# Where the q and k rows of one batch are transposed: TensorE or DMA, in an attention and MLP kernel

## The chip, the cores and the metric

The kernel runs on one core of a Trainium2 chip. The metric is the device time of one execution in microseconds (us). The core's engines are TensorE (PE, with its weight loads listed apart as PEld), VectorE (DVE), ScalarE (ACT), GpSimd (POOL) and SyncE (SP). Each works through its own queue in program order and waits on semaphores for the others. Loads are issued by POOL here, stores and DMA transposes by SP.

## The reference

Inputs are q, k and v of shape (8, 8, 576, 64), batch by head by position by head dimension, and two weight matrices of 512 x 2048 and 2048 x 512, all in float32.

```python
scores = (q @ k.T) / 8
mask_local = (rel >= 0) & (rel < 32)                       # heads 0..3
mask_strided = (rel >= 0) & (col % 32 == row % 32)         # heads 4..7
x = softmax(where(mask, scores, -1e9)) @ v                 # (8, 8, 576, 64)
x = x.transpose(0, 2, 1, 3).reshape(4608, 512)
out = relu(x @ w_in) ** 2 @ w_out                          # (4608, 512)
```

`rel` is the row's position less the column's. Heads 0 to 3 see the last 32 positions, heads 4 to 7 every 32nd one.

## The kernel before

**The MLP sets the rhythm.** The 4608 tokens are cut into nine chunks of 512. A chunk has 32 groups of four matmuls of 128x128 by 512 columns: 16 groups of the first product (`mm1`, line 709), then 16 of the second (`mm2`, line 731). So group 32c + i is step i of chunk c. After a group of mm1, ACT takes the rectified result out of PSUM (line 715) into one of four `r` tiles and DVE squares it (line 716). After every fourth group of mm2, ACT copies a tile `y` out (line 735) and SP stores it (line 739).

**Attention is threaded between the groups by hand.** The string `PLAN` gives, for each group number, the steps that are issued ahead of that group. Nothing reorders them: an engine's queue holds its instructions in the order in which the steps stand in `PLAN`. A chunk needs the attention of the tokens that it covers: chunk 2, from group 64 on, needs batch 2 (tokens 1152 to 1727), chunk 3, from group 96 on, batch 3.

**Units.** A pair of heads is a unit, numbered 4 x batch + pair: pairs 0 and 1 are local, 2 and 3 strided. Units 8 and 9 are batch 2's local pairs, units 12 and 13 batch 3's.

**The steps of a local unit:**

- *Load of q and k.* For batches 1 to 3 the step `l` (`load_qk_local_sw`, line 292) brings q or k of four heads in one DMA of 288 KB, six tokens in a row per partition, into columns of `xt` that are free at the time. `c` (`cast_qk_local`, line 299) rearranges a unit's part into a tile `q_l` or `k_l` of 96 partitions; the last letter names the engine (`a` ACT, `v` DVE). `T` (`step_T`, lines 455 and 462) transposes it with six PE transposes of 96 columns into a PSUM bank, from which ACT or DVE copies it to `qT` or `kTl`.
- From batch 4 on, `Q` (`load_qk_rows`, line 280) loads `q_l` or `k_l` directly, one token in a row, by two DMAs of 72 KB, one for each head. `Y` (`transpose_local`, line 380) issues two DMA transposes on SP, q first and then k. There are four buffers of `q_l` and four of `k_l`.
- *The rest.* `V` (`load_v_local_all`, line 420) loads the local v of a batch. `S` computes the scores (line 507), ACT their exponentials (line 523), and DVE multiplies them with the mask (line 529). `D` multiplies with v (line 669) and DVE divides (lines 674 and 675) into `x_l`. `E` transposes that into `xt`, from batch 2 on by a DMA transpose on SP (line 684).

**The steps of a batch's strided heads:** `C` (line 351) loads q or k rows into one tile for q and one for k, which every batch reuses. `X` (`transpose_str`, line 356) is their DMA transpose on SP into `qT_s` or `kT_s`. `k` (`step_K`, lines 367 and 370) spreads `kT_s` into the block matrix `kb`, one step for each of two halves. `U` (lines 392 and 395) loads v and `B` (line 399) spreads it into `vb`. `s` (`step_SS`, line 576, parts 0 to 2) computes the scores and `x` (`step_XX`, lines 587 and 590) the output, which DVE multiplies into `xt` (lines 600 and 606). With a batch number behind it, `X2k` is batch 2's transpose of k, `C3q` batch 3's load of q, `k30v` the first half of batch 3's spread of k, on DVE.

`o` (line 431) loads a quarter of the second weight matrix, and `m` clears a tile. An exclamation mark at `S` asks for all four exponentials at once.

Of the kernel before, what the change touches and what calls it, by code (L numbers as in the profile page):

```python
# [24 lines left out]
1: r1q mv1g  # L25
3: o0 mk1g
4: r1k V1
5: o1 U1 l2k8+9 mbg
6: o2 mv0g o3 mk0g V2
10: c4qv  # L30
11: c4kv
12: c5qv l2q8+9 T4qa
13: c5ka T4kv T5qa
14: W1q0v T5ka
15: S4
16: W1q1v
17: W1k0a W1k1v
18: S5! k10v
19: C2q C2k k11v D4.0
20: s1.0 D4.1 B10v  # L40
21: s1.1 D5.0
22: B11v l3k12+13 s1.2 U2
23: D5.1 x1.0
24: E4a
25: x1.1
26: X2k l3q12+13
27: x1.2
28: V3 E5a
29: c9kv
# [3 lines left out]
35: T8kv  # L53
37: T9kv
38: T8qv C3k
41: S8! k20v
42: T9qa B20v k21v
43: B21v
44: S9! D8.0 U3
45: D8.1  # L60
47: E8 D9.0
48: Q16k s2.0
49: D9.1
50: Q17q Q16q c12kv s2.1
51: c12qa E9 s2.2
52: Q17k c13kv c13qa
54: x2.0
55: X3q X3k
56: x2.1 C4k C4q
57: T12ka  # L70
58: V4 T13qv T12qa
59: T13ka
60: x2.2 B30v
61: B31v
63: U4 S12!
# [908 lines left out]
```

## Time and profile before

| what | us |
|---|---|
| median of three runs (301.77, 302.58, 1074.6) | 302.58 |
| the profiled execution | 301.36 |
| its span, from first to last instruction | 299.7 |
| matmuls of mm1 in the chain of waits (36% of the span) | 108 |
| matmuls of mm2 in the chain of waits (41% of the span) | 122 |
| ACT, line 715, 144 times | 85.5 |
| DVE, line 716, 144 times | 60.4 |

The page of the profile gives the share of busy time of each engine, the span in 40 slices, the DMA queues, the chain of work that ended last, and the costliest groups of instructions. The slices of PE, of its granted clock and of the DMA engines:

```profile
PE   7999999999999999999999999999999999999996
PEclk9999999999999999999999999999999999999999
DMA  7999999997999999999997998611011110010012
```

A digit is the share in tenths, and a slice is 7.5 us long. PE is busy throughout and has its full clock. The DMA engines are busy for the first 25 slices, in which all of q, k, v and the weights are loaded, and mostly idle after that. DMA transposes, loads and stores share them:

```profile
q0 software_dynamic: 54448, 18.82, 63.5%
q1 hardware_dynamic: 38512, 18.03, 30.0%
```

The columns are packets, MB, and the time that the packets took as a share of 16 engines' span. q0 holds POOL's loads, q1 the stores and the DMA transposes of SP.

In the lists of the trace, a line gives the start in us, the time in us, the engine, the line of the program, the operation, output and inputs, and in square brackets how long the engine was idle just before and what ended that.

### The profile page before, as it was taken

The page shows a single profiled execution, that of the slowest core. Times are in us where ns is not written, and L with a number is a line of the kernel's source. Part 1 is how long each engine was busy: PE and PEld are TensorE (multiplying, and loading weights), DVE is VectorE, ACT ScalarE, POOL GpSimd, SP SyncE. Part 2 cuts the span into 40 slices and gives each one's busy share as a digit, 9 for nine tenths or more (in the row PEclk, how much of TensorE's full clock was granted, in tenths as well). Part 3 has the DMA queues.
Part 4 walks back from the last instruction along what each step waited for, and adds up shares of the span by engine and source line. Part 5 has one row for each costly group of instructions (what it writes and reads, how often), then busy time and mean ns, then how long its engine had stood idle before and what let it go on. Part 6 is the DMA issues. An engine that isn't in the chain of part 4 may idle for free.

```text
span 299.7 us, 5685 instructions
## 1 busy us (share of the span) xinstructions
PE 292.3 (98%) x2172; PEld 145.7 (49%) x2172; DVE 180.2 (60%) x461; ACT 172.2 (57%) x324; POOL 71.7 (24%) x105
## 2 busy tenths in 40 slices
PE   7999999999999999999999999999999999999996
PEld 2554555544545444454454545444454444444444
DVE  5768699669668696589257945685485525104400
ACT  3758856685668744773467546645665356226511
POOL 8863933008204018047202900000000000000000
PEclk9999999999999999999999999999999999999999
DMA  7999999997999999999997998611011110010012
GB/s 146 190 210 201 191 200 185 157 231 112 141 131 182 172 156 199 151 141 179 204 162 112 161 205 119 108 56 71 35 23 39 67 56 0 35 72 36 0 70 72
DMA packets 93131, 37.28 MB, mean 124 GB/s; under 512 B 78956, under 2 KB 87238, under 8 KB 93104
## 3 DMA queue, kind: packets, MB, share of 16 engines
q0 software_dynamic: 54448, 18.82, 63.5%
q1 hardware_dynamic: 38512, 18.03, 30.0%
q8 instruction: 17, 0.28, 0.4%
q14 instruction: 10, 0.08, 0.1%
q10 hardware_dynamic: 144, 0.07, 0.1%
HBM read 38.21 MB, written 9.44 MB: 159 GB/s over the span
## 4 chain that ended last, share of the span: by engine, by line
PE 86%; DMA 5%; DVE 4%; issue 2%; ACT 1%; POOL 1%; DVEq 0%; ACTq 0%; POOLq 0%
PE psb L731 41%; PE psb L709 36%; DMA kT_s<-k_t 3%; DMA xt<-in_k_dram 2%; PE psb L669 2%; ACT r L715 1%; PE psb L590 1%; PE psb L576 1%; PE psb L756 1%; PE psb L587 1%; PE psb L552 1%; DVE x_l L657 1%; PE psb L455 1%; PE psb L507 1%; DVE g_sb L716 1%
## 5 line engine op out<-in xcount | busy, mean ns | idle before, releaser
L709 PE MATMUL psb<-xt,w_in_b 128*128 128x512 bf16 x576 | 133.5, 379 | 0.2 <-ACT r L715 0.2
L731 PE MATMUL psb<-w_out_b,g_sb 128*128 128x512 bf16 x560 | 128.2, 379 | 0.0
L715 ACT ACTIVATE r<-psb 128x512 bf16<-128x512 f32 x144 | 85.5, 600 | 39.6 <-PE psb L709 36.2
L716 DVE TENSOR_TENSOR g_sb<-r 128x512 bf16<-128x512 bf16 x144 | 60.4, 423 | 74.1 <-ACT r L715 73.5
L709 PEld LDWEIGHTS <-w_in_b 128*128 128x128 bf16 x576 | 53.3, 98 | 59.0 <-issue 1.5
L731 PEld LDWEIGHTS <-g_sb 128*128 128x128 bf16 x560 | 51.7, 98 | 57.1 <-DVE g_sb L716 0.3
L735 ACT COPY y<-psb 128x512 f32<-128x512 f32 x35 | 20.7, 590 | 53.6 <-PE psb L731 51.7
L600 DVE TENSOR_TENSOR xt<-psb,rv 64x144 bf16<-64x144 f32 x84 | 34.0, 405 | 8.2 <-ACT rv L593 7.1
L592 ACT ACTIVATE rv<-psb 128x432 f32<-128x432 f32 (+1 forms) x21 | 10.5, 500 | 10.4 <-PE psb L587 10.4
L675 DVE TENSOR_TENSOR x_l<-psb,rinv 96x384 bf16<-96x384 f32 x28 | 15.5, 553 | 1.0
L351 POOL DMA_DIRECT2D q_t<-in_q_dram x6 | 3.2, 539 | 48.2 <-DMA qT_s<-q_t 43.7
L606 DVE TENSOR_TENSOR xt<-psb,rv 64x270 bf16<-64x270 f32 (+1 forms) x28 | 10.9, 431 | 3.8 <-ACT rv L593 3.6
L577 ACT ACTIVATE e<-psb 128x432 bf16<-128x432 f32 (+1 forms) x21 | 10.4, 496 | 3.7 <-PE psb L576 3.7
L280 POOL DMA_DIRECT2D k_l<-in_k_dram x16 | 11.9, 748 | 2.5 <-PE psb L590 1.4
L280 POOL DMA_DIRECT2D q_l<-in_q_dram x16 | 11.6, 728 | 0.7 <-DMA k_t<-in_k_dram 0.7
L563 ACT ACTIVATE e<-psb 128x384 bf16<-128x384 f32 x24 | 9.6, 509 | 3.4 <-PE psb L552 3.4
L593 ACT ACTIVATE rv<-rv 128x432 f32<-128x432 f32 (+1 forms) x21 | 11.2, 533 | 0.7
L669 PEld LDWEIGHTS <-e 128*128 128x128 bf16 x168 | 8.5, 101 | 6.2 <-DVE e L529 1.9
L420 POOL DMA_DIRECT2D vl<-in_v_dram x7 | 10.1, 1438 | 4.6 <-DMA vl<-in_v_dram 3.7
L559 DVE TENSOR_TENSOR e<-e,mask_all 128x576 bf16<-128x576 bf16 x16 | 6.7, 458 | 6.3 <-ACT e L563 6.3
L669 PE MATMUL psb<-vl,e 128*128 128x65 bf16 x168 | 9.5, 195 | 0.9 <-DVE e L529 0.9
L351 POOL DMA_DIRECT2D k_t<-in_k_dram x6 | 3.2, 536 | 28.2 <-DMA kT_s<-k_t 27.3
(118 smaller groups left out, 218.0 us busy)
## 6 DMA issues: line engine op xcount, KB each, us to landing
out_dram<-y SPq DMA_DIRECT2D x35, 256.0 KB, 2.9
vl<-in_v_dram POOLq DMA_DIRECT2D x7, 384.0 KB, 9.5
w_out_b<-in_moe_w_out_dram POOLq DMA_DIRECT2D x4, 512.0 KB, 15.1
q_t<-in_q_dram POOLq DMA_DIRECT2D x7, 288.0 KB, 5.7
k_t<-in_k_dram POOLq DMA_DIRECT2D x7, 288.0 KB, 5.7
v_st<-in_v_dram POOLq DMA_DIRECT2D x7, 216.0 KB, 7.9
w_in_b<-in_moe_w_in_dram POOLq DMA_DIRECT2D x2, 704.0 KB, 13.4
k_l<-in_k_dram POOLq DMA_DIRECT2D x16, 72.0 KB, 6.4
```

The costliest lines, as they stand in the source:

```text
L280: nc.gpsimd.dma_start(out=t[:, :, hh, :], in_=src[b, 2 * p + hh].rearrange("(t p) d -> p t d", p=QL))
L592: nc.scalar.activation(rv, pn, AF.Ln)
L593: nc.scalar.activation(rv, rv, AF.Exp, scale=-1.0)
L600: nc.vector.tensor_tensor(to[:, :, NJ * part:NJ * (part + 1), par], of, by, op=ALU.mult)
L606: nc.vector.tensor_tensor(t, of[:, g:, :, lo:lo + k], by[:, g:, :, lo:lo + k], op=ALU.mult)
L669: nc.tensor.matmul(po[0:m, n, :], e[:, c:c + m], rhs[:, NL * part + n, 0:D + 1], start=True, stop=True)
L675: nc.vector.tensor_tensor(x, po[0:QL, :, 0:D], rinv[0:QL].to_broadcast([QL, NL, D]), op=ALU.mult)
L709: nc.tensor.matmul(ph, w_in_b[:, kk, 128 * ff:128 * (ff + 1)], xt[kk][:, 512 * c:512 * (c + 1)], start=(kk == order[0]), stop=(kk == order ...
L715: nc.scalar.activation(r, ph, AF.Relu)
L716: later(1, lambda: nc.vector.tensor_tensor(g[:, ff, :], r, r, op=ALU.mult))
L731: nc.tensor.matmul(py, g[:, ff, 128 * j:128 * (j + 1)], w_out_b[:, ff, :], start=(ff == 0), stop=(ff == 15))
L735: nc.scalar.copy(y, py)
```

## The change

Only `PLAN` changes; line numbers behind it go down by one.

```diff
-5: o1 U1 l2k8+9 mbg
-6: o2 mv0g o3 mk0g V2
+5: o1 U1 mbg
+6: o2 l2k8+9 mv0g o3 mk0g
-11: c4kv
-12: c5qv l2q8+9 T4qa
-13: c5ka T4kv T5qa
+11: c5qv
+12: c4kv l2q8+9 T4qa T5qa
+13: c5ka T4kv
-19: C2q C2k k11v D4.0
+19: C2q C2k V2 k11v D4.0
-22: B11v l3k12+13 s1.2 U2
+22: B11v Q12k Q13k s1.2 U2
-26: X2k l3q12+13
+26: X2k Q12q Q13q
-41: S8! k20v
-42: T9qa B20v k21v
-43: B21v
-44: S9! D8.0 U3
-45: D8.1
-47: E8 D9.0
+40: Y12
+41: S8!
+42: T9qa Y13
+44: S9! D8.0 k20v
+45: D8.1 k21v
+46: B20v
+47: E8 D9.0 B21v U3
-50: Q17q Q16q c12kv s2.1
-51: c12qa E9 s2.2
-52: Q17k c13kv c13qa
+50: Q17q Q16q s2.1
+51: E9 s2.2
+52: Q17k
-57: T12ka
-58: V4 T13qv T12qa
-59: T13ka
+58: V4
```

- Batch 3's local q and k: two loads of 288 KB (`l3k`, `l3q`), four casts and four PE transposes with their copies go. Eight row loads of 72 KB (`Q12k` to `Q13q`) stand in the places of the two loads, and four DMA transposes (`Y12`, `Y13`) are issued on SP ahead of groups 40 and 42.
- Batch 2: its spreads of k and v move from groups 41 to 43 to groups 44 to 47, and `U3`, which loads into the tile that they free, from 44 to 47. Its local v (`V2`) moves on POOL from behind the weights to behind `C2q` and `C2k`. Its load `l2k` moves behind `o2`.
- Batch 1: the cast of unit 5's q now stands ahead of the cast of unit 4's k, and unit 5's q is transposed one group earlier.

## The prediction

> **What bounds the kernel now.** I read the busy shares first, then the waits of TensorE (PE), then the chain of waits, then time lines of the stretches that the change touches.
>
> The first part of the page, then the line of PE's waits that counts (total, times, longest):
> ```profile
> PE 292.3 (98%) x2172; PEld 145.7 (49%) x2172; DVE 180.2 (60%) x461; ACT 172.2 (57%) x324; POOL 71.7 (24%) x105
> ```
> ```profile
> PE psb L669 <- DVE e L529: 0.9, 2, 0.6
> ```
> PE streams almost without a break, so time can come from only two places: matmuls taken out of its stream, and the few places where it stands still. Behind the first 20 us the one large standstill is the second line: twice, 0.9 us in sum, matmuls of `step_D` wait for DVE's masks. DVE's own time line shows why the masks were late, and PE's where it hurt:
> ```profile
> 61.70 0.42 DVE L716 TENSOR_TENSOR g_sb<-r 128x512 bf16<-128x512 bf16 x1 [0.44 <-ACT r L715]
> 63.84 0.38 DVE L367 COPY kb<-kT_s 64x864 bf16<-64x864 bf16 x1 [1.71 <-DMA kT_s<-k_t]
> 64.14 0.23 DVE L370 COPY kb<-kT_s 64x324 bf16<-64x324 bf16 x1
> 64.29 0.45 DVE L529 TENSOR_TENSOR e<-e,mask_all 128x576 bf16<-128x576 bf16 x1
> ```
> ```profile
> 66.59 0.35 PE L669 MATMUL psb<-vl,e 128*128 128x65 bf16 x6 [0.56 <-DVE e L529]
> ...
> 68.99 0.37 PE L669 MATMUL psb<-vl,e 128*128 128x65 bf16 x6 [0.32 <-DVE e L529]
> ```
> `k20v` (L367) stands in DVE's queue ahead of batch 2's masks and waits 1.71 us for the DMA transpose of k (X2k).
>
> The chain of waits, where batch 3's transposes run:
> ```profile
> 79.53 0.26 PE psb L455 x6
> 79.79 0.86 PE psb L731 x4
> 80.65 0.51 PE psb L455 x12
> 81.16 0.86 PE psb L731 x4
> 82.03 0.26 PE psb L455 x6
> ```
> 24 transposes of 96 columns stand on the path itself, 0.26 us for six.
>
> **The change, part by part.**
>
> *TensorE's transposes of units 12 and 13 go.* 0.26 + 0.51 + 0.26 = 1.03 us off PE's stream. With them go five ACT instructions (two casts of 0.82, three copies of 0.64: 3.6 us) and three of DVE (0.57, 0.35, 0.76: 1.7 us). PE waits for neither engine in 72 to 92 us, so I count these at nothing.
>
> *Batch 2's spreads go from groups 41 to 43 to groups 44 to 47.* `k20v` comes three groups (3 x 0.86 = 2.6 us) later. Its DMA comes earlier too: issue start plus time to landing, from the DMA view asked one issue at a time, gives landings at 41.8 (l2k), 44.3, 46.8 (two parts of w_out), 50.2 (V2), 51.8 (l2q), 53.5 (C2q) and 55.2 (C2k), one after the other. The V2 step is 3.4 us, and V2 now stands behind C2q and C2k, so C2k lands near 51.8, and X2k, which SP issued at 55.27 as C2k landed, starts 3.4 us earlier. 2.6 + 3.4 against a wait of 1.71 leaves 4.3 us of margin: the 0.9 us of standstill go. V2 itself then lands at 55 to 60; its user D8.0 runs at 64.8. U2 waits behind the row loads on POOL, landing near 60 instead of 58.5; its spread is at group 46, near 66.
>
> *q casts first.* At 30.2 PE's weight load waited 0.2 for c5qv, which stood behind c4kv. I take 0.15.
>
> Sum so far: 1.03 + 0.9 + 0.15 = 2.1 us, the most that I can find.
>
> *What is added.* Eight row loads of 72 KB for two loads of 288 KB, and four DMA transposes (Y12, Y13) at groups 40 and 42. None is on PE; all are on 16 DMA engines that the page shows nine tenths busy until about 185 us. The old loads: landing steps of 1.5 (55.2 to 56.7) and 0.9 (58.5 to 59.4), 2.4. The new rows, by batch 5's eight: from 118.8 to 122.4 in seven steps, 0.51 each, 4.1. Rows add 1.7 us. A local transpose costs 0.6 us where no load runs beside it (batch 4's landed at 104.6, 105.2, 105.8), and up to 2.5 beside loads: between C3k's landing at 74.4 and the last row load's at 91.2 lie 16.8 us, of which U3 takes 1.8 (as U2), eight row loads 4.1, a store 0.8, and four transposes the rest. So four add 2.4 to 10.1, and all together 4.1 to 11.8 us of DMA work.
>
> [...]
>
> *Queues.* On POOL every issue starts only when the DMA eight issues before it has landed (24.76 after 24.5, 50.75 after 50.2), so eight small issues push U2 back by some 5 us and V3 from 50.75 to 57 or so; V3's user D12.0 is at 88.1. On SP, Y12 waits for rows that land near 60 to 62, with Y13, E8, E9 and the stores behind it. E8 had its data at 69.99 and E9 at 73; I expect SP past Y13 at 67 to 69. If that cover went, E8 and E9 (landing at 80.1 and 81.7) would still have 5.5 us until group 64 at 87.2. S12 at 86.0 needs Y12, issued near 62; with the 8 to 12 us of its neighbours it lands by 75.
>
> **Where the gain can stick.** The next late thing is X3k, the same transpose for batch 3, which `k30v` at group 66 waits for already:
> ```profile
> 90.73 0.38 DVE L367 COPY kb<-kT_s 64x864 bf16<-64x864 bf16 x1 [0.26 <-DMA kT_s<-k_t]
> ...
> 92.60 0.24 DVE L370 COPY kb<-kT_s 64x324 bf16<-64x324 bf16 x1
> ```
> ```profile
> 94.27 0.36 PE L576 MATMUL psb<-qT_s,kb 128*128 128x54 bf16 x8
> ```
> X3k lands at 90.7 (80.16 + 10.5), both spreads are done 2.1 us later (92.84), and PE takes s3.0 at 94.27. With 2.1 us gained PE is there at 92.2. Call d how much later X3k lands than 90.7: PE then loses d + 0.6, and the net change is d - 1.5 us, or -2.1 if d is below -0.6. What is d? Work of 4.1 us at the low price meets room here:
> ```profile
> 66.00:68.00 2.00, 1.44 (x13) 0.78 (x13) 1.90 (x6) 0.94 (x3) 0.00 (x0) 1.00 0.74 218
> 68.00:70.00 2.00, 1.68 (x14) 0.70 (x12) 1.95 (x6) 1.04 (x2) 1.80 (x4) 1.00 0.33 35
> ...
> 76.00:78.00 2.00, 2.00 (x18) 1.07 (x17) 0.47 (x2) 1.09 (x2) 0.72 (x1) 1.00 4.19 54
> ```
> Of these stretches the last two columns are the DMA share and GB/s. From 66 to 70 about 1.8 us of DMA time are idle, because C3q waited on POOL for X2q's landing. So 2.3 us are left at the low price, 10 at the high one. Against that X2 starts 3.4 us earlier, C3's loads follow it, and at 54 GB/s (76 to 78) it isn't the volume that decides. With C3 early enough, d reaches -0.8. I take d = +0.5, a little under the middle of -0.8 and 2.3, because Y12 and Y13 lie nearer to the thin stretch at 66 to 70 than to the crowded one.
>
> **Forecast.** -1.5 + 0.5 = -1.0 us. The profiled execution took 301.36 (span 299.7 and 1.7 around it), so 300.4. The runs shown beside it are 301.77, the median 302.58, and 1074.6, which I leave aside; the mean of the three ordinary times is 301.9, 0.5 above the profiled one. So 300.9.
>
> **Rivals.**
> 1. *X3k takes over the wait that X2k had.* For it: the DMA engines are full, added work is up to 11.8 us, k30v waits already. Against: the idle time at 66 to 70. It decides from d = 1.5: at d = 2.3 the time is 0.8 us above before (302.7 on the median's scale), at d = 4, 2.5 above (304.4). Chance 0.25.
> 2. *The same, at the full price:* d = 7.5 to 10 gives 6 to 8.5 us, 308 to 310.5. Against: no load that the trace shows is displaced so far. Chance 0.07.
> 3. *The full gain, with no price for the transposes.* If one costs no more than its 0.6 us and fits wholly into the idle time, X3k lands earlier and 2.1 us stay: 299.3 to 299.8. Chance 0.14. [...]
> 4. *It doesn't do what it says:* X2k still lands after `k20v`, because V2's and batch 3's rows now run beside it, the standstill stays, and of the 1.2 us that are left d takes most: within 0.5 us of before, 301.4 to 302.4. Chance 0.07.
> 5. Over 6 us faster: no row holds so much. 0.02.
>
> The forecast, net -1.8 to -0.3 (300.1 to 301.6), has 0.45.
>
> **The numbers.** Two per cent, about what a measurement of this kernel can tell from no change, is 6 us. Faster by more 0.02, slower by more 0.07 (rival 2), within 0.91. Range: from the full gain with some scatter below the profiled time (298.9) to d = 4 with 0.3 us of scatter (304.7); rivals 2 and 5 and the end of rival 1 lie outside. Faster at all has 0.6, so the forecast's own range of 300.1 to 301.6 stands beside it.
>
> **What would show it.** Right: 24 matmuls fewer at L455; no wait of L367 for kT_s near 64; no wait of L669 for DVE near 66 to 69; X2k issued near 52; group 64 some 2 us earlier. d is read from X3k's landing and from a wait ahead of L576 near 92. Wrong: a PE wait for kb, for kTl or for xt between 84 and 95, or SP still at Y13 when E8's data is there.

## The result, and the profile after

The changed kernel took 305.74 us (median of six runs, 303.25 to 309.07), the kernel before 301.47 in six runs beside it. The ratio is 1.0115, with a 95% interval of 1.0070 to 1.0159: some 3.5 us slower, and within 2%. The predicted 300.9 and its range (to 304.7) lie below that, and the forecast was 1.0 us faster, not slower. The ratios, not the medians, leave out every execution that is more than 1.5% above the fastest of its kernel, here those of 309.07 and 1074.6.

The profiled execution took 306.8 us (span 305.1), against 301.36 (299.7) before: 5.4 us more of span. Line numbers are one lower than before, so mm1 is L708, mm2 L730, the scores of the strided heads L575. The busy shares, the slices of PE, its clock and the DMA engines, and the two DMA queues of the page after:

```profile
PE 291.1 (95%) x2112; PEld 145.9 (48%) x2148; DVE 177.7 (58%) x458; ACT 169.5 (56%) x319; POOL 77.5 (25%) x111
...
PE   7999999999968999999999999999999999999994
...
PEclk9999999999979999999999999999999999999998
DMA  8999999999999989999999999622111110011012
...
q0 software_dynamic: 58384, 18.82, 60.2%
q1 hardware_dynamic: 40944, 18.62, 33.5%
```

PE has less to do (291.1 against 292.3 us), in a longer span. Of the 60 matmuls fewer, 24 are the transposes that went, as among the weight loads (PEld, 2148 against 2172); the other 36 records are missing from this trace. Slices 12 and 13 (84 to 99 us) were full before and now hold a 6 and an 8, and the granted clock dips to 7. The two queues have 3936 and 2432 packets more: the row loads and the transposes. PE's waits (total, times, longest):

```profile
PE psb L708 <- DMA xt<-x_l: 2.6, 1, 2.6
...
PE psb L575 <- DVE kb L366: 1.0, 1, 1.0
...
PE psb L589 <- DVE vb L398: 0.6, 1, 0.6
...
PE psb L454 <- DVE q_l L298: 0.4, 1, 0.4
```

The wait of `step_D` for the masks (L669, 0.9) is gone, and four others are new. The largest is mm1 at group 64 waiting for E9's transpose (L683). DVE's time line at batch 2's spread of k shows why the old one went:

```profile
66.47 0.55 DVE L674 TENSOR_TENSOR x_l<-psb,rinv 96x384 bf16<-96x384 f32 x1
66.94 0.37 DVE L366 COPY kb<-kT_s 64x864 bf16<-64x864 bf16 x1
67.23 0.23 DVE L369 COPY kb<-kT_s 64x324 bf16<-64x324 bf16 x1
67.39 0.45 DVE L528 TENSOR_TENSOR e<-e,mask_all 128x576 bf16<-128x576 bf16 x1
```

Nothing stands in brackets behind L366: X2k, issued at 51.31 instead of 55.27, had landed at 61.68, and the spread waits for nothing. The same spread for batch 3 is now what waits:

```profile
96.16 0.38 DVE L366 COPY kb<-kT_s 64x864 bf16<-64x864 bf16 x1 [3.04 <-DMA kT_s<-k_t]
```

The chain of waits of the changed kernel, where it leaves PE (start, us, what):

```profile
81.95 2.67 SPq L355
...
84.71 11.43 DMA kT_s<-k_t
...
96.16 0.38 DVE kb L366
...
98.17 0.38 PE psb L575 x8
```

`SPq L355` is SP's issue of X3q, which stands ahead of X3k: C3k had landed at 82.06, but SP was at X3q until 84.62. X3k was issued at 84.71 instead of 80.16 and landed at 96.1 instead of 90.7. So d of the prediction is 5.4, where 0.5 was taken. Ahead of it, PE's time line at group 64, and the stretches around it (PE, PEld, DVE, ACT and POOL busy; then granted clock, DMA share, GB/s):

```profile
88.64 1.44 PE L708 MATMUL psb<-xt,w_in_b 128*128 128x512 bf16 x3 [2.56 <-DMA xt<-x_l]
```
```profile
87.00:88.00 1.00, 0.00 (x0) 0.00 (x0) 0.27 (x1) 0.00 (x0) 0.00 (x0) 1.00 3.26 84
88.00:89.00 1.00, 0.36 (x1) 0.10 (x1) 0.00 (x0) 0.00 (x0) 0.00 (x0) 0.69 0.29 30
89.00:90.00 1.00, 1.00 (x6) 0.42 (x5) 0.00 (x0) 0.00 (x0) 0.00 (x0) 0.50 1.62 146
90.00:91.00 1.00, 0.85 (x8) 0.52 (x8) 0.26 (x1) 0.60 (x1) 0.00 (x0) 0.50 1.60 159
91.00:92.00 1.00, 0.92 (x3) 0.39 (x3) 0.91 (x3) 0.00 (x0) 0.00 (x0) 0.60 1.66 160
92.00:93.00 1.00, 1.00 (x11) 0.51 (x8) 0.30 (x1) 0.67 (x2) 0.00 (x0) 1.00 2.19 60
```

PE stands for 2.56 us, and then runs for some 3 us at half its clock.

**Where the 5.4 us are.** The starts of the groups in the two traces, after less before:

| up to the start of | difference, us | what lies in the step |
|---|---|---|
| group 44 | +0.74 | waits for q_l (L454) and vb (L589) |
| group 48 | -0.49 | the standstill at the masks, 1.23 with both its pieces |
| group 64 | -1.52 | 24 PE transposes, 1.04 |
| group 68 | +2.74 | 2.56 wait for E9, and 1.7 by the lower clock |
| group 72 | +3.92 | the wait for X3k (1.0) |
| last group | +4.3 | kTl of a later batch, 0.4 |
| end | +5.4 | the last three stores took 2.4 to 3.9 us each to land, before 1.6 to 1.7 (as in both repeats below, so this is of the execution) |

Up to group 64 the change gains 1.5 us. Then it loses 5.4 within eight groups, to two transfers that come late. Landings, in us (issue start plus time to landing, from the DMA view):

| transfer | before | after |
|---|---|---|
| V3 issued | 50.75 | 56.0 |
| V3 landed | 65.7 | 73.4 |
| Y12q, Y12k, Y13q, Y13k | none | 69.8, 72.7, 76.2, 83.4 |
| C3q, C3k | 72.9, 74.4 | 80.3, 82.1 |
| E8, E9 | 80.1, 81.7 | 84.5, 88.6 |
| X3q, X3k | 87.3, 90.7 | 93.2, 96.1 |

C3q, which X3q and then X3k wait for, is 7.5 us late in two nearly equal steps. It stands behind V3 in POOL's queue: V3's last rows come through at 73.42, and the first of the 4 KB packets behind them starts at 73.01, 3.6 us later than before (69.44). From there to the landing it is 7.3 us, where it was 3.4.

### The profile page after: what moved, and what is told of

The parts are those of the page before. It is cut to its first block, busy times and chain, and to the rows that moved or that the text cites. A ratio compares the mean times of both kernels' runs of the same rounds, so it can differ in the third digit from the quotient of the medians.

```text
span 305.1 us, 5610 instructions
## 1 busy us (share of the span) xinstructions
PE 291.1 (95%) x2112; PEld 145.9 (48%) x2148; DVE 177.7 (58%) x458; ACT 169.5 (56%) x319; POOL 77.5 (25%) x111
## 4 chain that ended last, share of the span: by engine, by line
PE 80%; DMA 7%; DVE 6%; ACT 2%; issue 2%; SPq 1%; DVEq 0%
PE psb L708 35%; PE psb L730 33%; DMA kT_s<-k_t 4%; DMA kTl<-k_l 3%; PE psb L765 1%; ACT r L714 1%; PE psb L589 1%; PE psb L668 1%; PE psb L755 1%; PE psb L454 1%; PE psb L575 1%; PE psb L586 1%; SPq L355 1%; DVE g_sb L715 1%; DVE vb L398 1%
## 5 line engine op out<-in xcount | busy, mean ns | idle before, releaser
L708 PE MATMUL psb<-xt,w_in_b 128*128 128x512 bf16 x557 | 133.4, 381 | 4.2 <-DMA xt<-x_l 2.6
L730 PE MATMUL psb<-w_out_b,g_sb 128*128 128x512 bf16 x543 | 125.5, 379 | 1.0 <-issue 0.2
L708 PEld LDWEIGHTS <-w_in_b 128*128 128x128 bf16 x576 | 53.6, 98 | 62.8 <-issue 5.7
L730 PEld LDWEIGHTS <-g_sb 128*128 128x128 bf16 x560 | 51.9, 98 | 57.7 <-DVE g_sb L715 0.3
L279 POOL DMA_DIRECT2D q_l<-in_q_dram x20 | 14.6, 734 | 9.5 <-DMA q_t<-in_q_dram 4.5
L279 POOL DMA_DIRECT2D k_l<-in_k_dram x20 | 14.9, 755 | 5.0 <-DMA w_out_b<-in_moe_w_out_dram 2.2
## 6 DMA issues: line engine op xcount, KB each, us to landing
q_t<-in_q_dram POOLq DMA_DIRECT2D x7, 288.0 KB, 12.6
```

The lines of the kernel that those rows point to most:

```text
L279: nc.gpsimd.dma_start(out=t[:, :, hh, :], in_=src[b, 2 * p + hh].rearrange("(t p) d -> p t d", p=QL))
L708: nc.tensor.matmul(ph, w_in_b[:, kk, 128 * ff:128 * (ff + 1)], xt[kk][:, 512 * c:512 * (c + 1)], start=(kk == order[0]), stop=(kk == order ...
L730: nc.tensor.matmul(py, g[:, ff, 128 * j:128 * (j + 1)], w_out_b[:, ff, :], start=(ff == 0), stop=(ff == 15))
```

## The experiments

The theory from the traces: what comes in the DMA engines between 52 and 95 us (rows, local transposes, V3, C3, E8, E9, X3) is more than they do in that time, so the last of them, and whoever needs it first, pays. Rivals: the rows alone do it (through POOL's queue); the transposes alone do it (through SP's queue or their cost); the moves of batch 2's steps do it; or this trace was a chance execution.

**Batch 3 back on TensorE, the rest of the change kept.**

```diff
-22: B11v Q12k Q13k s1.2 U2
+22: B11v l3k12+13 s1.2 U2
-26: X2k Q12q Q13q
+26: X2k l3q12+13
-40: Y12
-42: T9qa Y13
+42: T9qa
-50: Q17q Q16q s2.1
-51: E9 s2.2
-52: Q17k
+50: Q17q Q16q c12kv s2.1
+51: c12qa E9 s2.2
+52: Q17k c13kv c13qa
-58: V4
+57: T12ka
+58: V4 T13qv T12qa
+59: T13ka
```

> Batch 3's q and k as in the kernel before (two loads of 288 KB, casts, TensorE's transposes); batch 2's later spreads, V2 behind C2q and C2k, and q casts first stay. Theory A (the four transposes, with what they cost on the DMA engines, delay E9 and X3k): E9 lands near 81, no wait of PE at group 64, the standstill near 66 to 69 stays away; 0.5 to 1 us faster than the kernel before. Theory B (the eight row loads fill POOL's eight places and push V3 and C3 back): the same number, for the rows are gone too. Theory C (the moves of batch 2 delay what follows): PE still waits at group 64, and the time stays 3 us or more above before.

Measured: 301.21 us, ratio 1.0003 (0.9974 to 1.0032). E9 landed at 81.7 and X3k at 90.8, as before; PE waits neither for masks near 67 nor for xt or kb behind it. The loss sits in batch 3's rows and transposes. The moves of batch 2 cost nothing behind group 44, and they are what took the standstill away (1.23 us from group 44 to 48). The gain of 0.5 to 1 us that was expected isn't there: this trace is 1.09 us late at group 44, 0.85 of it from the first group on.

**Only the rows: loaded as in the change, transposed by TensorE.**

```diff
-40: Y12
-42: T9qa Y13
+42: T9qa
-58: V4
+57: T12ka
+58: V4 T13qv T12qa
+59: T13ka
...
-        copy(dst.rearrange("c (p j) -> c p j", j=6), pt.rearrange("c (j p) -> c p j", j=6))
+        if u // 4 == 3:
+            copy(dst, pt)
+        else:
+            copy(dst.rearrange("c (p j) -> c p j", j=6), pt.rearrange("c (j p) -> c p j", j=6))
```

> As the changed kernel, with the eight row loads, but units 12 and 13 are transposed by TensorE again (groups 57 to 59). Theory A: V3 and C3 as late as in the changed kernel at their issue (V3 near 56), yet E9 lands by 83 and X3k by 92; PE doesn't wait at group 64; time within 1 us of before. Theory B: C3q lands near 80 and E9 after 86 as in the changed kernel; PE waits 1 us or more at group 64; 3 us or more above before.

Measured: 300.73 us, ratio 0.9979 (0.9957 to 1.0000). V3 is issued at 56.13, as late as in the changed kernel, and yet it lands at 69.1, and C3q at 72.0, E9 at 81.4 and X3k at 89.9. Rows and a late V3 alone delay nothing that PE needs.

**Only the transposes: the two wide loads and the casts of before, then Y12 and Y13.**

```diff
-22: B11v Q12k Q13k s1.2 U2
+22: B11v l3k12+13 s1.2 U2
-26: X2k Q12q Q13q
+26: X2k l3q12+13
-40: Y12
+40: c12kv c12qa Y12
-42: T9qa Y13
+42: T9qa c13kv c13qa Y13
```

Tokens stand in another order in this kernel's q and k of batch 3, so its scores of that batch are others than the reference's; the work is the same.

> The two loads of 288 KB and the casts as before (casts at groups 40 and 42), but DMA transposes Y12 and Y13 in place of TensorE's. q and k positions of units 12 and 13 stand in another order, so their scores are others than the reference's. Theory A: E9 lands at 86 to 90 and PE waits at group 64 as in the changed kernel, 3 to 5 us above before. Theory B: V3 issues near 51 and C3q lands by 76, E9 by 83, no wait at group 64, within 1 us of before.

Measured: 302.49 us, single times of 300.1 to 306.1, ratio 1.0009 (0.9979 to 1.0040). In the trace V3 is issued at 49.4 and still lands at 72.3, and Y13k lands at 77.2, E9 at 82.4, X3k at 92.1; PE waits 0.4 us for kb. Transposes alone bring the lateness near, and on the median not over the edge; three times of ten at 305.7 to 306.1 suggest that some executions go over it.

**The same DMA work as in the change, less E8's and E9's transposes, which TensorE does.**

```diff
-47: E8 D9.0 B21v U3
-48: Q16k s2.0
+47: D9.0 B21v U3
+48: Q16k s2.0 E8a
-51: E9 s2.2
-52: Q17k
+51: s2.2
+52: Q17k E9a
...
-        if b >= 2:
+        if b >= 3:
```

> The changed kernel with units 8 and 9's outputs transposed by TensorE (12 transposes, 0.5 us) in place of the DMA transposes E8 and E9. Every theory: no wait for xt at group 64 and no dip of the clock at 88 to 92. If group 64 is what set the time (2.6 us of standstill and 1.7 of lower clock), 3 us or more faster than the changed kernel. If X3k's landing is the bound behind it (96.1 in the changed kernel), PE comes earlier to s3.0 and waits there for 3 to 5 us instead, and the time is within 1.5 us of the changed kernel, unless X3k also lands earlier because two transposes fewer stand ahead of it: each us earlier is a us of time.

Measured: 301.12 us, ratio 0.9988 (0.9960 to 1.0016). Y13k lands at 79.1, C3q at 77.9, X3k at 90.1, and no wait is left at group 64 or ahead of L575. With batch 3's rows and transposes all there, two transposes fewer are enough on the median, so neither part of the change is late by itself: what decides seems to be the sum of the DMA work. One execution of a later kernel with the same DMA work was late even so (304.49, under the loss at the start).

**The changed kernel again, with no edit, in two further jobs.** First:

> The changed kernel once more, for a second profile. If the standstill at group 64 belongs to the kernel and not to one execution, E9 lands at 86 or later again, PE waits for xt there and X3k lands after 93; the time is 303 to 307. If the first profile was an odd one, E9 lands by 84 and the wait is gone, and the time is nearer to 302.

Measured: 305.95 us, ratio 1.0101 (1.0039 to 1.0164). Y13k lands at 82.3, C3k at 83.7, E9 at 86.3 and X3k at 96.0 in its trace. So E9 and X3k are late as expected, but PE comes to group 64 with E9, and the wait is at L575, 4.4 us. The profiled execution is the slowest of the four (311.31): near 150 us PE waits once more, 2.5 us for batch 5's `kTl`. Second:

> The changed kernel a third time, for one more profiled execution. If the lateness is of the kernel: E9 lands after 84 us and X3k after 93.5 us again, and PE waits for xt, kb or kTl between 84 and 100 us, by 2 us or more in sum. If it comes and goes with the execution: E9 near 82 and X3k near 91.6 as in the execution with the dummy matmuls, no such wait, time 300 to 301.

Measured: 308.79 us in its one, profiled, execution. Y13k lands at 85.1, E9 at 90.0, X3k at 97.2. Its waits of PE:

```profile
PE psb L708 <- DMA xt<-x_l: 3.9, 2, 2.1
...
PE psb L551 <- DMA kTl<-k_l: 0.6, 1, 0.6
```

So the lateness is of the kernel, and which of its transfers PE meets first changes with the execution. The granted clock, which is on record for every execution, points the same way. In the three profiled executions it was half for 3.4 us or more at a standstill (see the end), and its mean over them is 0.988 to 0.992. A mean of 0.995 or less stands with nine of the changed kernel's eleven executions, and with 9 of the 87 of the kernel before that were timed beside the experiments.

**Y12 and Y13 behind E8, E9 and X3 on SP, unit 12's and 13's later steps eight groups back.**

```diff
-40: Y12
-42: T9qa Y13
+42: T9qa
-56: x2.1 C4k C4q
+56: x2.1 C4k C4q Y12 Y13
-63: U4 S12!
+63: U4
-65: D12.0
-67: Y16 D12.1 S13! X4k C5q k31v
+67: Y16 X4k C5q k31v
-71: s3.0 E12 Q20k Q21q Q20q
+71: S12! s3.0 Q20k Q21q Q20q
-73: D13.0 D13.1
-75: E13
-77: s3.2
+73: D12.0
+75: D12.1 S13!
+77: E12 s3.2
-80: x3.0 B40v
-81: B41v
+80: x3.0 B40v D13.0
+81: B41v D13.1
+83: E13
```

> The changed kernel with Y12 and Y13 moved behind E8, E9, X3q and X3k on SP (group 56), and batch 3's local scores and outputs eight groups later (S12 at 71, S13 at 75, D12 and D13 at 73 to 81). The DMA work is the same; only its order differs. Theory A (what stands ahead of E9 and X3k in SP's queue delays them): E9 lands by 83 and X3k by 92, no wait at group 64, 0.5 to 2 us faster than before. Theory B (the small row loads delay everything on the engines, whatever the order): E9 lands after 85 and PE waits at group 64; 2 us or more slower than before.

Measured: 304.01 us, ratio 1.0087 (1.0052 to 1.0121). E9 lands at 81.0 and X3k at 90.8, on time, but Y12k at 92.8 and Y13k at 95.7. Its waits of PE (its lines are two lower than before's; L505 is the scores of the local heads, L550 those of a later batch):

```profile
PE psb L505 <- DMA kTl<-k_l: 1.7, 1, 1.7
...
PE psb L550 <- DMA kTl<-k_l: 1.0, 1, 1.0
```

Neither theory had the time: the first had E9 and X3k right, but not who would wait instead. The order on SP chooses who waits; it doesn't remove the work. **V3 later, behind C3 and U3 on POOL:**

```diff
-28: V3 E5a
+28: E5a
-47: E8 D9.0 B21v U3
+47: E8 D9.0 B21v U3 V3
```

> The changed kernel with V3 (3072 rows of 128 bytes) moved on POOL from group 28 to behind C3q, C3k and U3 (group 47), so that it doesn't run beside Y12 and Y13. If the rows of V3, pushed into the time of Y12 and Y13 by the eight small loads, are what slows those transposes, the four land by 72 (69.8 to 83.4 in the changed kernel), C3q by 73, E9 by 84, and PE's wait at group 64 goes: 2 to 4 us faster than the changed kernel. If the transposes cost their time anyway, Y13's k lands after 78 and the wait stays.

Measured: 303.89 us, ratio 1.0045 (1.0012 to 1.0078). The four transposes land at 67.2, 69.1, 71.5 and 74.8 (changed kernel: 69.8 to 83.4), C3q at 73.0, E9 at 80.0, X3k at 92.4. V3 lands at 88.0, and its user waits:

```profile
PE psb L668 <- DMA vl<-in_v_dram: 1.4, 1, 1.4
```

V3's 3072 rows beside the transposes made those slow: the first three land 5.0 to 5.9 us after their issue here, and 7.4 to 10.7 in the six traces that have V3 beside them. It works the other way too: V3, issued near 56, landed at 69.1 and 69.8 with no transposes of batch 3 beside it, and at 73.4 to 77.1 in five of those six. The fourth transpose is another matter: 8.0 us here, and from 8.2 to 17.4 in the six (see the trough at the end). The forecast of 72 for the last landing and of 2 us against the changed kernel isn't shown: the intervals of the ratios overlap, and this profile is of the fastest of ten executions. Put elsewhere, V3 is late itself.

**What the lateness is worth: thirteen matmuls, 2.8 us of PE work that no output uses, ahead of group 64.**

```diff
-64: X4q
+64: X4q w13
...
-            pw = bank("py")
+            pw = bank("py" if "py" in banks else "pt")
```

> The changed kernel with 13 more matmuls of 512 columns (2.8 us, their result is not used) ahead of group 64, so that PE has work while it waits for E9. If the lower clock after the standstill (0.5 to 0.7 of full from 88 to 92, some 1.7 us lost) sets the time, it stays at full and the kernel gets 1.5 us faster than the changed one. If X3k's landing is the bound, PE only waits longer for kb at s3.0 (2.5 to 3 us in place of 1.0) and the time stays within 0.7 us. If E9 lands earlier than PE gets there, the 2.8 us are simply added.

Measured: 303.66 us, ratio 1.0082 (1.0045 to 1.0119): not slower than the changed kernel, in spite of 2.8 us more work. So on the median some of it runs where PE would stand anyway; how much is not shown, since the only profiled execution (302.9 us) is one without such a wait: E9 at 82.0, X3k at 91.6, no wait for either, and the 2.8 us simply added (group 64 at -1.69, the groups behind it at +1.11 against before). Up to group 64 the program is the changed kernel's, so this is one more execution of its first 87 us, in which the DMA engines were on time. Less the 2.8 us it is 300.1, or 1.3 below the profiled 301.36 of before. The stretches (columns as above) show what differed; first the changed kernel, then this one:

```profile
72.00:74.00 2.00, 1.95 (x18) 0.94 (x15) 1.93 (x7) 1.00 (x3) 1.42 (x3) 1.00 2.50 173
74.00:76.00 2.00, 2.00 (x18) 1.09 (x17) 0.19 (x1) 0.68 (x2) 2.00 (x4) 1.00 0.26 15
76.00:78.00 2.00, 2.00 (x20) 0.97 (x16) 0.93 (x3) 1.15 (x3) 0.65 (x1) 1.00 0.88 135
```
```profile
72.00:74.00 2.00, 2.00 (x16) 0.96 (x15) 1.93 (x7) 1.09 (x3) 1.59 (x3) 1.00 1.13 192
74.00:76.00 2.00, 2.00 (x18) 1.06 (x17) 0.02 (x1) 0.68 (x2) 2.00 (x4) 1.00 1.14 216
76.00:78.00 2.00, 2.00 (x18) 1.03 (x17) 1.11 (x3) 1.15 (x3) 1.92 (x3) 1.00 1.24 160
```

From 74 to 76 us the DMA engines of the changed kernel moved 15 GB/s, with Y13k, C3q and C3k issued and not landed; here 216.

**The loss at the start.** The kernel with E8 and E9 on TensorE, and in addition the old order of the casts and V2 behind U2:

```diff
-11: c5qv
-12: c4kv l2q8+9 T4qa T5qa
-13: c5ka T4kv
+11: c4kv
+12: c5qv l2q8+9 T4qa
+13: c5ka T4kv T5qa
-19: C2q C2k V2 k11v D4.0
+19: C2q C2k k11v D4.0
-22: B11v Q12k Q13k s1.2 U2
+22: B11v Q12k Q13k s1.2 U2 V2
```

> As in the kernel with units 8 and 9 transposed by TensorE at step E, and in addition the order of batch 1's q and k casts as before and V2 behind U2 on POOL, so that its 3072-row issue no longer stands beside DVE's spread of batch 1's v. Theory (the start of the changed kernel loses 0.9 us, of which 0.6 by DVE's slowed spread and 0.3 by the order of the casts; from group 4 on the kernel without E8 and E9 as transposes gains 1.5): no PE wait for vb near 44, group 24 no later than before, end 1.5 to 2.5 us ahead of before, ratio about 0.993 to 0.996. Rival (the slowing isn't POOL's issue, or V2 behind U2 comes too late for D8.0 at 64 or meets another DVE copy): start as late as before this edit or a PE wait at D8.0, ratio 0.998 to 1.002.

Measured: groups 4 to 44 within 0.2 us of before, no wait for vb, and group 64 at -1.77. Both reasons for the start's loss stand. From the time lines: DVE's copy and POOL's issue in the changed kernel, then the same copy here:

```profile
40.89 1.06 DVE L398 COPY vb<-v_st 54x1408 bf16<-54x1408 bf16 x1
```
```profile
40.19 1.44 POOL L419 DMA_DIRECT2D vl<-in_v_dram  x1 [0.48 <-DMA v_st<-in_v_dram]
```
```profile
40.75 0.52 DVE L398 COPY vb<-v_st 54x1408 bf16<-54x1408 bf16 x1
```

How much this costs depends on where the copy meets the issue. In eight traces it starts with 0.24 us or more of V2's issue to run, and in all eight it ends 0.32 or 0.33 us after the issue's end, having taken 0.57 to 1.39: the copy is held until POOL is done.

The whole time was missed all the same: 301.02 us, ratio 0.9998 (0.9969 to 1.0027). Its profiled execution, the slowest of its twelve (304.49), shows 22 GB/s from 74 to 76 us, Y13k at 80.5 and X3k at 93.7, so a wait of 2.45 us for kb and 1.1 for kTl. In that execution the gain of the start was there and was lost to late transfers behind it; why the median doesn't show it either stays open, since the other eleven have no profile. The last version has batch 3 wholly on TensorE, batch 2's later spreads, `l2k` behind `o2` as in the change, the casts in the old order and V2 behind U2:

> Batch 3 wholly as before (wide loads, TensorE transposes), batch 2's spreads later as in the change, order of casts as before, V2 behind U2 on POOL. Theory: the standstill of 0.9 us at groups 46 and 47 is gone and nothing is lost at the start, so 0.9 to 1.2 us ahead of before, ratio 0.996 to 0.997. Rival (the later spreads or V2 cost elsewhere): ratio 0.999 to 1.002.

Measured: 300.58 us, ratio 0.9990 (0.9960 to 1.0021). Of the gain expected, 1.07 us are there in its profile from group 48 to group 120; then one wait for batch 5's transposes, which come late in that execution (302.59, the second slowest of twelve), takes it away:

```profile
PE psb L552 <- DMA kTl<-k_l: 2.1, 1, 2.1
```

No version was shown to beat the kernel before.

## Why the prediction was wrong, point by point

- *TensorE's transposes, 1.03:* right, 1.04 from group 48 to 64.
- *The standstill at the masks, 0.9:* right, and a little more (1.23). X2k landed at 61.68, five microseconds ahead of its spread, and the kernel with only the moves of batch 2 has the same gain.
- *q casts first, 0.15:* wrong in sign. In its place stands a wait of 0.39 us for q_l (L454), and the order of before takes it away.
- *V2 behind C2q and C2k, counted at its landing alone:* incomplete. POOL's issue of V2 now falls beside DVE's spread of batch 1's v, which takes 1.06 instead of 0.51, and PE waits 0.55 for it. The prediction followed V2 through the queue and not the engine time of its issue.
- *Added DMA work, 4.1 to 11.8 us:* not contradicted, though the upper end is too high: it counts X3q and X3k (288 KB each) like local transposes of 144 KB, and with time taken by size (an estimate) four of these add 6.7, so 8.4 in all; what surfaced is 5.4 at X3k, of which none shows with rows alone (89.9) and 1.4 with transposes alone (92.1). The two prices don't add: V3's 3072 rows and the four transposes slow each other, as the kernel with V3 later shows, and the small rows put V3 later still (issued at 56.0 against 49.4 without them).
- *d = +0.5, the step that failed.* It was taken between -0.8 and 2.3, the room that the low price leaves, because 1.8 us of DMA time were idle from 66 to 70. By the time that these microseconds came, Y12, Y13 and V3 filled them and more; the same stretches in the changed kernel (share 0.74 and 0.33 before):

```profile
66.00:68.00 2.00, 2.00 (x15) 1.02 (x15) 1.97 (x7) 1.72 (x6) 0.22 (x1) 1.00 1.45 227
68.00:70.00 2.00, 1.95 (x23) 1.08 (x21) 1.92 (x7) 1.27 (x3) 0.86 (x2) 1.00 1.78 165
```

  Nor did the earlier X2 make C3 early: X2k landed 2 us sooner, but X2q at 67.2 as before, so C3q was issued at 67.78 instead of 68.19. It landed 7.5 us later, half of it behind V3 in POOL's queue, which the prediction followed to V3's own user only. The other half, C3q's slow packets, has no known cause. The rule behind d, d - 1.5, was right in form: 5.4 - 1.5 is 3.9, and group 72 stands at +3.92.
- *E8's and E9's 5.5 us of cover:* gone, the second step that failed. SP was past Y13 at 68.8, as forecast, but E9 behind it, issued at 73.69 (73.03 before), landed 6.9 us later: issued on time isn't served on time. PE paid 2.56 there, before X3k, and 1.7 more at the lower clock, which no term of the sum had.
- *Rival 1* is what happened, at a d beyond the 4 at which the range was cut off. *Rival 3* did not occur: beside loads the four transposes of 144 KB landed 7.8, 8.6, 10.0 and 15.8 us after their issue, and X2k in the trace of before 8.5. The load C3q took 12.6 us to land as well; what failed is the price of 0.6 us, which was taken where no load ran. *Rivals 2 and 4* did not occur.
- The forecast of -1.0 describes the execution in which the DMA engines were on time (-1.3, worked out above). In the three of the changed kernel that were profiled they were not (306.8, 308.79 and, in the first repeat, 311.31), and the median of 305.74 is nearer to those.

## What to carry to other kernels

Work moved from a full engine to DMA queues that are nine tenths busy is not free because its own user has time; here E9 landed 6.9 us later and X3k 5.4. List every transfer that lands behind it in either queue, with the margin of each, and count the smallest margin, not the sum of the idle time. Ask also what the longest load, when it is pushed back by small ones, will run beside. A gain that rests on a margin of one or two microseconds is lost in those executions in which the transfers are a little later: here X3k had 1.5 us before it cost more than the change gained, and it landed 5.4, 5.3 and 6.5 us later than before in three executions of the changed kernel.

## What the runs showed of the hardware

- **The clock fell after some standstills and not after others.** In the first trace of the changed kernel, where PE stood for 2.56 us, the granted clock was half for 3.4 us (the stretches from 88 to 92 us above). In the second repeat, which has 1.8 and then 2.1 us without a matmul, it was half for 6.8 us, from 89 to 95.8. In the first repeat, which has 4.39 us, it was half for 3.4 us from 97.5 on; with a second long wait, of 2.5 us near 150, its mean over 309.5 us is 0.988, so some 7.4 us of half clock in all. Where PE waited 2.45 us in the kernel with the start undone it stayed at 1.00, and in the last version, with a wait of 2.1 us, its mean is 1.000; PE's time line of the former and the stretch in which the standstill ends:

```profile
95.69 0.37 PE L575 MATMUL psb<-qT_s,kb 128*128 128x54 bf16 x8 [2.45 <-DVE kb L366]
```
```profile
94.00:96.00 2.00, 0.31 (x9) 0.31 (x10) 1.92 (x8) 0.60 (x1) 1.78 (x3) 1.00 0.76 209
```

  So a fall is on record with 2.56 us, and none with 2.45; what decides is not shown.
- **Two kinds of packets share the engines.** By counts of the packets that start in a microsecond, 128-byte rows alone went at some 1150 (1218 from 97 us on in the kernel before; 1063 and 1223 from 102 and 103 in the changed one), the transposes' 256-byte packets alone at some 1000 (998 from 103 and 932 from 110, in the same order), both together at some 400 each (404 and 417 from 83, 404 and 421 from 64). With 400 of each, that is about three quarters of what either did alone.
- **A trough in the DMA engines.** Between 70 and 80 us, seven traces have microseconds in which packets of under 60 KB start, though loads are waiting: two in the kernel before (76 to 78), three, three and six in the changed kernel's, five in the one with the start undone, and one each in the kernel with the thirteen matmuls and in the one with E8 and E9 on TensorE. The engines are not idle there: in the changed kernel's trace fourteen packets of 4 KB that start between 73.3 and 74 us take 3.2 to 3.8 us each, where 0.32 is usual. Packets of 4 KB that take over 1.5 us between 66 and 82 us number 14, 27 and 26 in the changed kernel's traces and 26 in that with the start undone, the four late ones; the kernels with the thirteen matmuls and with E8 and E9 on TensorE have 5 and 0, and the kernel before has none. The same program to that point ran with and without them, so their number is a matter of the execution. What causes them stays open, and with it why the changed kernel's times spread from 302.6 to 311.3.
